# Attention scores of a gated linear attention: full-height products of a bank first, half-height products after

## The chip, the cores and the metric

The kernel runs on one core of a Trainium2 chip. The metric is the device time in microseconds of one execution; the kernel before was run three times. One further execution was taken with the hardware profiler, and all rows below come from its trace.

## The reference

Three stages follow each other: a gated linear attention over 4 x 8 heads, 768 tokens and 48 features; a gated product with shared weights; and a second layer in which each of the 3072 tokens goes to one of eight experts.

```python
# attention: q, k, v, f_logit are [4, 8, 768, 48]
f = 1.0 / (1.0 + np.exp(-f_logit))
for t in range(S):
    state = f[:, :, t, :, None] * state + np.einsum('bhd,bhe->bhde', k[:, :, t], v[:, :, t])
    y[:, :, t] = np.einsum('bhd,bhde->bhe', q[:, :, t], state)
# first MoE: x is y as [3072, 384], w_a and w_b [384, 1536], w_out [1536, 384]
x = ((x @ w_a) * (x @ w_b)) @ w_out
# second MoE: the expert of a token is the argmax of x @ w_gate, E = 8, F = 1024
for e in range(E):
    h = np.maximum(x[mask] @ w1[e], 0.0)
    out[mask] = gate_w[mask, None] * eom[mask, e, None] * (h @ w2[e])
```

## The kernel before, in words

**Tiles.** The 3072 tokens are 24 tiles of 128: six chunks of each of the four sequences. A tile goes through 14 steps of attention, and two tiles make a block of the first MoE. Numbers that need float32 precision are held as a high and a low part, so that most products come in three.

**One tile of attention.** The eight heads stand in four pairs. The step `a_z` writes the decayed q and k in half precision into the tile `z`: of a pair, q's high part twice for each head, q's low part, k high and low, k low and high. Each part has 64 columns per head, 48 of them used. A DMA transpose (L667) turns `z` into `zT`, in which a pair's two heads stand on the lower and the upper 64 partitions, or a head's high and low parts on both.

**The scores.** `a_score(i, u)` makes the scores of the four heads with number u in their pairs. They fill one bank of PSUM: four stretches of 128 columns, one for each pair j, in the bank tile `ps_at`. Each stretch is the sum of two products. L726 multiplies k (high and low, on all 128 partitions) with q's high part that stands on both halves: a product over 128 rows of TensorE's array. L727 multiplies k's high part on 64 of the partitions with q's low part on the same 64: a product over 64 rows. In the trace the former has the form 128*128, the latter 64*128. Both load weights of their own first (LDWEIGHTS, engine PEld in the profile).

**What follows a bank.** VectorE multiplies it with the causal mask into `sm` (L729), ScalarE makes the high part `Sh` (L731), VectorE the low part `Sl` (L732). L742 to L744 multiply these with v (`a_av`), L758 and L760 bring in the state before the chunk (`a_inter`), and L698 to L700 update the state (`a_kv`). The last of these use half of the array's columns, form 128*64.

**The first MoE.** `m_ab` (L816 to L818) multiplies a block with two column tiles of the weights, 256 columns at a time; `m_out` (L840 to L842) multiplies the result with `w_out`, 400 columns at a time.

**Order.** The first six tiles and first two blocks are laid out by a table of nominal times, while weights arrive and are decoded. From then on a loop over blocks j and weight tiles f calls `m_ab`, `m_out` and, by a table of steps, the attention of tiles 2j+2 and 2j+3. A scheduler then sets the order within each engine; it may put other work between two instructions of the program. Each engine works strictly through its list.

Of the kernel before, what the change touches and what calls it, by code (L numbers as in the profile page):

```python
# [18 lines left out]
DRAM = bass.MemoryType.DRAM  # L19
# [3 lines left out]
def general_path(nc, tc, q, k, v, f_logit, w_a, w_b, w_out, w_gate, w_ogate, w1, w2, out, cons):  # L23
    """the whole computation again, for values that the fast path doesn't carry"""
# [11 lines left out]
    with ExitStack() as ctx:  # L36
# [9 lines left out]
        # ---- recurrence over the tokens, one by one  # L46
# [52 lines left out]
        # ---- first MoE and the routing, 128 tokens at a time  # L99
        with tc.tile_pool(name="g_m1", bufs=1) as sp:  # L100
# [4 lines left out]
            for nm, w, n, m in (("a", w_a, KD, FF), ("b", w_b, KD, FF), ("o", w_out, NF, DM)):  # L105
                wt[nm] = tl("g_w" + nm, [P, n, m])
                for kk in range(n):
                    for c in range(m // DM):
                        cs = slice(c * DM, (c + 1) * DM)
                        src = w[kk * P : (kk + 1) * P, cs]  # L110
                        dst = wt[nm][:, kk, cs]
                        if w.dtype != I64:
                            nc.sync.dma_start(dst, src)
                            continue
                        raw = tl("g_raw", [P, DM, 2], I32)
                        nc.sync.dma_start(raw.bitcast(I64).rearrange("p f c -> p (f c)"), src)
                        top, low = raw[:, :, 1], raw[:, :, 0]
                        ei = tl("g_ei", [P, DM], I32)
                        ef = tl("g_ef", [P, DM])
                        mi = tl("g_mi", [P, DM], I32)  # L120
                        bits = dst.bitcast(I32)
                        nc.vector.tensor_scalar(
                            out=ei, in0=top, scalar1=20, scalar2=0x7FF,
                            op0=ALU.logical_shift_right, op1=ALU.bitwise_and,
                        )
                        nc.vector.tensor_copy(out=ef, in_=ei)
                        nc.vector.tensor_scalar(
                            out=ef, in0=ef, scalar1=896.0, scalar2=0.0, op0=ALU.subtract, op1=ALU.max
                        )
                        nc.vector.tensor_scalar(out=ef, in0=ef, scalar1=254.0, scalar2=None, op0=ALU.min)  # L130
                        nc.vector.tensor_copy(out=ei, in_=ef)
                        nc.vector.tensor_scalar(
                            out=ei, in0=ei, scalar1=23, scalar2=None, op0=ALU.logical_shift_left
                        )
                        nc.vector.tensor_scalar(
                            out=mi, in0=top, scalar1=3, scalar2=0x7FFFFF,
                            op0=ALU.logical_shift_left, op1=ALU.bitwise_and,
                        )
                        nc.vector.scalar_tensor_tensor(
                            out=mi, in0=low, scalar=29, in1=mi,  # L140
                            op0=ALU.logical_shift_right, op1=ALU.bitwise_or,
                        )
                        nc.vector.tensor_tensor(out=mi, in0=mi, in1=ei, op=ALU.bitwise_or)
                        nc.vector.scalar_tensor_tensor(
                            out=bits, in0=top, scalar=-(1 << 31), in1=mi,
                            op0=ALU.bitwise_and, op1=ALU.bitwise_or,
                        )
                        # below float32's range: zero
                        nc.vector.tensor_scalar(
                            out=ef, in0=ef, scalar1=1.0, scalar2=None, op0=ALU.min  # L150
                        )
                        nc.vector.tensor_tensor(out=dst, in0=dst, in1=ef, op=ALU.mult)
# [94 lines left out]
        # ---- the experts, 128 slots at a time  # L247
# [57 lines left out]
def kernel(  # L305
# [46 lines left out]
    # ---------------------------------------------------------------- pools  # L352
# [17 lines left out]
    # ------------------------------------------------------------ constants  # L370
    # n(t): number of steps of the static slope up to token t of a chunk
# [72 lines left out]
    # routing state: (token, scale) per token, counts, sums of the softmax, ranges  # L444
# [9 lines left out]
    # DRAM scratch: rows of the first MoE by token (and a row of zeros), slot table  # L454
# [6 lines left out]
    # ---------------------------------------------------- weights, hi and lo  # L461
# [16 lines left out]
    def decoded(raw, n, on_pool):  # L478
        """384 columns of a weight as float32, times 2^WS"""
# [7 lines left out]
        # The upper word as a float has the double's exponent over 8. Times 2^(WS - 126) its  # L487
        # three upper exponent bits are clear, as long as the double is below 2^(128 - WS):
        # the sums tell. Below 2^(-112 - WS) it comes to nothing.
# [34 lines left out]
    def conv_o(f, raw, n, on_pool):  # L524
# [7 lines left out]
        # w_out @ [w_gate | w_output_gate] for these rows  # L532
# [18 lines left out]
    # -------------------------------------------------------------- attention  # L551
# [15 lines left out]
    # Heads in pairs, the first of a pair on the lower 64 partitions and the second on the upper:  # L567
    # of a pair, q hi twice for each head, q lo, k hi and lo, k lo and hi
# [11 lines left out]
    def part(o):  # L580
        """the partitions of the pairs' first or second heads"""
        return slice(64 * o, 64 * o + D)
# [27 lines left out]

    def squares(i, n, src, scale, junk):
        """the sum of squares of every token's row"""
        nc.scalar.activation(
            out=junk, in_=src, func=AF.Square, scale=scale, accum_out=st_qkv[:, i, n : n + 1]
        )
# [55 lines left out]
    def a_u(i):  # L671
        """the state before this chunk, hi and lo"""
# [43 lines left out]
    def a_score(i, u):  # L716
# [6 lines left out]
        for j in range(4):  # L723
            half = slice(64 * u, 64 * u + 64)
            k2, ql = T[:, 5 * j + 3 + u], T[half, 5 * j + 2]
            nc.tensor.matmul(sc[:, j], k2, T[:, 5 * j + u], start=True, stop=False)  # L726
            nc.tensor.matmul(sc[:, j], k2[half], ql, start=False, stop=True)  # L727
# [38 lines left out]
    def a_turn(i):  # L766
        """rows to columns by DMA, two bytes at a time: the words' lower and upper halves apart"""
# [37 lines left out]
    # -------------------------------------------------------------- first MoE  # L805
# [81 lines left out]
    def r_rank(j):  # L887
        """every token's slot: its expert's base and the tokens before it"""
# [19 lines left out]
    def free_order(key, ins):  # L908
        """scatters of one table go to rows of their own: they don't wait for each other"""
# [50 lines left out]
    # ------------------------------------------------------- experts' weights  # L960
# [3 lines left out]
    def load_expert(e, g, part):  # L964
        """two f-tiles of the e-th expert in line: part 0 of w1, part 1 of w2"""
# [23 lines left out]
    # --------------------------------------------------- program, first phase  # L989
# [10 lines left out]
    def route(j, f):  # L1000
        """the tokens of block j, sent to their experts in steps"""
# [50 lines left out]
    # the first two blocks run while the weights come: emission by nominal time  # L1052
# [41 lines left out]
    # -------------------------------------------------------------- second MoE  # L1094
    # The experts stand in a line: first the one with the most tokens before the last block, then
    # the others by their number of tokens, most first, each place with slots of its own number.
    # No token of the last block goes to the first half of the first place's slots, so these can
    # start before that block ends.
# [14 lines left out]
    def tiles_of(e):  # L1113
        """tiles of the e-th place: first slot and size"""
# [12 lines left out]
    def choose_first():  # L1127
        """the expert with the most tokens before the last block gets the first place"""
# [24 lines left out]
    def first_tokens(n):  # L1153
        """half n of the first place's slots"""
# [17 lines left out]
    def e_turn(e, u):  # L1172
        """rows to columns by DMA, two bytes at a time: the words' lower and upper halves apart"""
# [50 lines left out]
    def e_h(e, f, n=None):  # L1224
        """the first product of the e-th place for f, or of half n of the first place"""
# [4 lines left out]
        # hi, then lo with the tokens of a pair first: both parts of these stand together  # L1230
# [17 lines left out]
    def is_pair(m):  # L1248
        """a tile so small that both parts of h stand beside each other in one product"""
        return m in (P // 4, P // 2)  # L1250
# [55 lines left out]
    def line_up(pc):  # L1306
        """the experts in their line, and whether one has too many tokens for its place"""
# [46 lines left out]
    def check_path():  # L1354
        """anything that the fast path doesn't carry: values out of its range or overfull experts"""
# [36 lines left out]
    def ahead(e, turn, columns, f):  # L1392
        """the input of the e-th place, while the one before is computed"""
# [6 lines left out]
    # ------------------------------------------------------------- the program  # L1400
# [137 lines left out]
```

## Time and profile before

| | |
|---|---|
| median of three runs | 931.11 us (930.51 to 933.27) |
| the profiled execution, its span | 931.4 us |
| mean granted TensorE clock | 0.974 of full speed |
| TensorE matmul busy | 862.8 us, 93%, 6733 instructions |
| VectorE, ScalarE, GpSimd busy | 549.6, 448.0 and 360.0 us |

A matmul's busy time holds its passage through the array, which overlaps that of the next one; how fast products follow each other is read from the distance of their starts. Times in rows are counted from the start of the profiled span. An arrow in brackets names what ended the engine's idle time before a row.

### The profile page before, as it was taken

How to read it: one execution, taken by the hardware profiler on the slowest of the kernel's cores; microseconds unless marked ns; L12 is line 12 of the kernel's file. 1: busy time of each engine (PE TensorE's matmuls, PEld its weight loads, DVE VectorE, ACT ScalarE, POOL GpSimd, SP SyncE). 2: the span in 40 equal slices, each digit the busy share in tenths (PEclk: the TensorE clock that was granted, in tenths of full speed). 3: DMA queues.
4: the chain of work that ended last, by engine and by line, in shares of the span. 5: the costliest groups of instructions: out<-in, count | busy, mean ns of one | idle time of the engine just before them, and what ended most of it. 6: DMA issues, size and time to landing. Idle time of an engine off the chain costs nothing.

```text
span 931.4 us, 18145 instructions
## 1 busy us (share of the span) xinstructions
PE 862.8 (93%) x6733; PEld 797.7 (86%) x6733; DVE 549.6 (59%) x1289; ACT 448.0 (48%) x1104; POOL 360.0 (39%) x428
## 2 busy tenths in 40 slices
PE   2689789989999999999999999999978999999993
PEld 1477789978989898989899999999878999999993
DVE  8887875554746474646555565642546666666630
ACT  6756655533545454536454554432424434445530
POOL 4444664352535353535445363412344231131111
PEclk9997999989999999999999999999989999999997
DMA  9874535462516252443526161211348644665610
GB/s 202 186 167 137 158 89 111 88 69 55 107 38 122 38 116 44 90 71 57 95 43 117 36 124 20 60 33 50 122 120 225 172 125 159 189 175 155 185 58 22
DMA packets 247756, 98.53 MB, mean 106 GB/s; under 512 B 210600, under 2 KB 243717, under 8 KB 247658
## 3 DMA queue, kind: packets, MB, share of 16 engines
q1 hardware_dynamic: 242538, 87.22, 42.3%
q0 software_dynamic: 4320, 10.03, 3.5%
q8 instruction: 55, 0.90, 0.4%
q14 instruction: 43, 0.35, 0.1%
q10 hardware_dynamic: 800, 0.02, 0.1%
HBM read 63.56 MB, written 10.49 MB: 80 GB/s over the span
## 4 chain that ended last, share of the span: by engine, by line
PE 70%; DMA 9%; DVE 8%; issue 7%; ACT 2%; POOL 2%; SPq 0%; POOLq 0%; DVEq 0%; ACTq 0%
PE ps_ab L816 9%; PE ps_ab L817 9%; PE ps_ab L818 9%; PE ps_out L301 5%; PE ps_out L842 4%; PE ps_out L841 4%; PE ps_yk L301 4%; PE ps_out L840 4%; PE ps_ab L1221 3%; PE ps_ab L1220 3%; PE ps_ab L1222 3%; PE ps_at L727 3%; PE ps_at L726 3%; DMA slots<-info,di 2%; DMA zT<-z 2%
## 5 line engine op out<-in xcount | busy, mean ns | idle before, releaser
L816 PE MATMUL ps_ab<-xh,wab 128*128 128x256 f32 x864 | 253.0, 293 | 5.5 <-DVE gf L824 3.8
L817 PE MATMUL ps_ab<-xl,wab 128*128 128x256 f32 x864 | 248.8, 288 | 0.5 <-DVE xl L797 0.5
L818 PE MATMUL ps_ab<-xh,wab 128*128 128x256 f32 x864 | 248.5, 288 | 0.2 <-POOL wab L520 0.2
L828 POOL TENSOR_TENSOR gl<-gf,gh 128x256 fp32r<-128x256 f32 x144 | 111.6, 777 | 244.7 <-ACT gh L827 243.3
L816 PEld LDWEIGHTS ps_ab<-xh,wab 128*128 128x128 f32 x864 | 167.1, 194 | 9.4 <-DVE gf L824 4.7
L817 PEld LDWEIGHTS ps_ab<-xl,wab 128*128 128x128 f32 x864 | 167.1, 193 | 2.3 <-DVE xl L797 1.8
L818 PEld LDWEIGHTS ps_ab<-xh,wab 128*128 128x128 f32 x864 | 167.2, 193 | 0.7 <-POOL wab L520 0.3
L824 DVE SCALAR_TENSOR_TENSOR gf<-ps_ab,asb 128x256 f32<-128x256 f32 x144 | 60.3, 419 | 81.4 <-ACT asb L823 76.0
L827 ACT ACTIVATE gh<-gf 128x256 fp32r<-128x256 f32 x144 | 59.9, 417 | 93.4 <-DVE gf L824 90.0
L841 PE MATMUL ps_out<-wo,gh 128*128 128x400 f32 x264 | 93.0, 352 | 2.2 <-DVE wo L547 2.2
L842 PE MATMUL ps_out<-wo,gl 128*128 128x400 f32 x264 | 92.2, 357 | 2.2 <-POOL gl L828 2.2
L840 PE MATMUL ps_out<-wo,gh 128*128 128x400 f32 x264 | 89.9, 348 | 1.3 <-ACT wo L546 1.3
L1294 POOL DMA_INDIRECT out_dram<-ys,tab x29 | 30.0, 1033 | 145.4 <-ACT ys L1289 139.9
L823 ACT ACTIVATE asb<-ps_ab 128x256 f32<-128x256 f32 x144 | 54.4, 379 | 58.1 <-PE ps_ab L818 57.9
L1221 PE MATMUL ps_ab<-xsl,wab 128*128 128x256 f32 (+5 forms) x216 | 73.5, 341 | 0.1
L1220 PE MATMUL ps_ab<-xsh,wab 128*128 128x256 f32 (+5 forms) x216 | 73.5, 341 | 0.1
L1222 PE MATMUL ps_ab<-xsh,wab 128*128 128x256 f32 (+5 forms) x216 | 73.3, 339 | 0.0
L977 DVE TENSOR_TENSOR wab<-raw,wab 128x768 fp32r<-128x768 f32 x48 | 46.6, 972 | 40.4 <-ACT wab L301 40.0
L1234 ACT ACTIVATE h<-ps_ab 128x256 fp32r<-128x256 f32 (+5 forms) x72 | 34.7, 483 | 69.3 <-PE ps_ab L1222 64.6
L1238 DVE SCALAR_TENSOR_TENSOR h<-ps_ab,h 128x64 fp32r<-128x64 f32 (+5 forms) x96 | 41.1, 450 | 36.7 <-ACT h L1234 36.7
L729 DVE TENSOR_TENSOR sm<-ps_at,mask 128x512 f32<-128x512 f32 x48 | 33.0, 688 | 45.0 <-PE ps_at L727 44.8
L732 DVE TENSOR_TENSOR Sl<-sm,Sh 128x512 f16<-128x512 f32 x48 | 33.9, 706 | 40.0 <-ACT Sh L731 40.0
(261 smaller groups left out, 1977.7 us busy)
## 6 DMA issues: line engine op xcount, KB each, us to landing
raw<-in_moe_w_dram SPq DMA_DIRECT2D x64, 384.0 KB
in_f<-in_f_logit_dram SPq DMA_DIRECT2D x24, 192.0 KB
in_q<-in_q_dram SPq DMA_DIRECT2D x24, 192.0 KB
in_k<-in_k_dram SPq DMA_DIRECT2D x24, 192.0 KB
in_v<-in_v_dram SPq DMA_DIRECT2D x24, 192.0 KB
raw<-in_moe_w_a_dram SPq DMA_DIRECT2D x12, 384.0 KB
raw<-in_moe_w_b_dram SPq DMA_DIRECT2D x12, 384.0 KB
raw<-in_moe_w_out_dram SPq DMA_DIRECT2D x12, 384.0 KB
```

The source lines that it names most:

```text
L301: return lambda *a, **k: tc.keep_in_program_order(op(*a, **k))
L816: nc.tensor.matmul(pab[:, a], wh[:, kk, o : o + P], xh[:, kk], start=(kk == 0), stop=False)
L817: nc.tensor.matmul(pab[:, a], wh[:, kk, o : o + P], xl[:, kk], start=False, stop=False)
L818: nc.tensor.matmul(pab[:, a], wl[:, kk, o : o + P], xh[:, kk], start=False, stop=(kk == KD - 1))
L824: nc.vector.scalar_tensor_tensor(out=gf, in0=pab[:, 1], scalar=2.0**-WS, in1=asb, op0=ALU.mult, op1=ALU.mult)
L828: nc.gpsimd.tensor_tensor(out=gl, in0=gf, in1=gh.bitcast(F32), op=ALU.subtract)
L840: nc.tensor.matmul(o, gh[:, ts], wh[:, u], start=(f == 0), stop=False)
L841: nc.tensor.matmul(o, gh[:, ts], wl[:, u], start=False, stop=False)
L842: nc.tensor.matmul(o, gl[:, ts], wh[:, u], start=False, stop=(f == NF - 1))
L1220: nc.tensor.matmul(ph, wh[:, kk, o : o + P], sh[:, kk, us], start=(kk == 0), stop=False)
L1221: nc.tensor.matmul(ph, wh[:, kk, o : o + P], sl[:, kk, us], start=False, stop=False)
L1222: nc.tensor.matmul(ph, wl[:, kk, o : o + P], sh[:, kk, us], start=False, stop=(kk == KD - 1))
```

## The change

In a bank the four products over 128 rows now come first, one for each pair, and the four products over 64 rows behind them. The first product clears the accumulation state of the bank (`start`), the last one closes it (`stop`); before, each stretch had a `start` and a `stop` of its own. Each product is tied behind the one before it by a dependency without a semaphore, so that the scheduler keeps the eight in this sequence. Comments and doc strings were dropped elsewhere in the file, which shifts line numbers: both products are now made in line 741.

```diff
+    def queued_behind(ins, before):
+
+        tc.add_manual_dep(
+            ins.ins,
+            before.ins.name,
+            mybir.DependencyInfo(mybir.DependencyClass.NoSync, mybir.DependencyReason.DATA),
+            reason="one group of a bank",
+        )
...
-        for j in range(4):
-            half = slice(64 * u, 64 * u + 64)
-            k2, ql = T[:, 5 * j + 3 + u], T[half, 5 * j + 2]
-            nc.tensor.matmul(sc[:, j], k2, T[:, 5 * j + u], start=True, stop=False)
-            nc.tensor.matmul(sc[:, j], k2[half], ql, start=False, stop=True)
+
+        half = slice(64 * u, 64 * u + 64)
+        before = None
+        for part in range(2):
+            for j in range(4):
+                k2, q2 = T[:, 5 * j + 3 + u], T[:, 5 * j + u]
+                if part == 1:
+                    k2, q2 = k2[half], T[half, 5 * j + 2]
+                first_of, last_of = part + j == 0, part + j == 4
+                ins = nc.tensor.matmul(sc[:, j], k2, q2, start=first_of, stop=last_of)
+                if before is not None:
+                    queued_behind(ins, before)
+                before = ins
```

TensorE's list around one bank of the loop over blocks, before: the last product of `m_ab`, then the bank's products over 128 rows (L726) and 64 rows (L727) in turn, then `a_av`.

```order
L816 MATMUL ps_ab<-xh,wab 128x256
L726 LDWEIGHTS zT
L726 MATMUL ps_at<-zT 128x128
L727 LDWEIGHTS zT
L727 MATMUL ps_at<-zT 128x128
L726 LDWEIGHTS zT
L726 MATMUL ps_at<-zT 128x128
...
L727 LDWEIGHTS zT
L727 MATMUL ps_at<-zT 128x128
L742 LDWEIGHTS Sh
```

The same place in the changed kernel; L741 makes all eight pairs of rows, of which the first four are over 128 rows and the last four over 64.

```order
L833 MATMUL ps_ab<-xh,wab 128x256
L741 LDWEIGHTS zT
L741 MATMUL ps_at<-zT 128x128
...
L741 LDWEIGHTS zT
L741 MATMUL ps_at<-zT 128x128
L759 LDWEIGHTS Sh
```

Only the sequence inside the bank moved; the rows ahead of it and behind it are the same. With line numbers matched, the lists of all five engines and the waits in them are otherwise as before.

One bank of the 48 (tile 20, u = 0) has other work inside. Before, its first three products stand ahead of a stretch of `m_ab` and `m_out`, the other five behind it. The start of the stretch and its end, before:

```order
L900 MATMUL ps_at<-oh,stri 128x8
L726 LDWEIGHTS zT
L726 MATMUL ps_at<-zT 128x128
L727 LDWEIGHTS zT
L727 MATMUL ps_at<-zT 128x128
L726 LDWEIGHTS zT
L726 MATMUL ps_at<-zT 128x128
L816 MATMUL ps_ab<-xh,wab 128x256
...
L842 MATMUL ps_out<-wo,gl 128x400
L727 LDWEIGHTS zT
L727 MATMUL ps_at<-zT 128x128
L726 LDWEIGHTS zT
```

In the changed kernel the same slots are taken, three products ahead and five behind:

```order
L917 MATMUL ps_at<-oh,stri 128x8
L741 LDWEIGHTS zT
L741 MATMUL ps_at<-zT 128x128
...
L833 MATMUL ps_ab<-xh,wab 128x256
...
L859 MATMUL ps_out<-wo,gl 128x400
L741 LDWEIGHTS zT
L741 MATMUL ps_at<-zT 128x128
```

The three ahead are now over 128 rows, and of the five behind the first is over 128 rows and four over 64.

## Rows read from the trace of the kernel before

**Rows 1.** Busy us (instructions) of each engine, clock, DMA share, GB/s by stage

```profile
0.00:130.00 130.00, 91.06 (x674) 73.78 (x674) 110.96 (x232) 83.14 (x229) 65.42 (x81) 0.93 0.69 167
130.00:616.00 486.00, 480.51 (x4315) 442.45 (x4316) 274.29 (x689) 239.64 (x639) 214.28 (x269) 0.99 0.41 74
```

**Rows 2.** Waits of PE, 130 to 616 us: total, times, longest

```profile
PE ps_yk L742 <- ACT Sh L731: 3.2, 1, 3.2
PE ps_at L726 <- DMA zT<-z: 1.2, 2, 0.7
```

**Rows 3.** Line L726 before 130 us and from 130 to 616: ns min/median/max

```profile
L726 PE MATMUL ps_at<-zT x32: 216/289/330, 18.4 to 76.1; 128*128 128x128 f16 x32
...
L726 PE MATMUL ps_at<-zT x160: 216/230/230, 146.3 to 609.8; 128*128 128x128 f16 x160
```

**Rows 4.** PE in order of time around one bank: start, duration, instruction

```profile
300.33 0.34 PE L840 MATMUL ps_out<-wo,gh 128*128 128x400 f32 x1
...
300.70 0.34 PE L842 MATMUL ps_out<-wo,gl 128*128 128x400 f32 x1
300.96 0.22 PE L698 MATMUL ps_at<-vs,z 128*64 128x48 f16 x2
...
301.33 0.19 PE L700 MATMUL ps_at<-vs,z 128*64 128x48 f16 x1
301.45 0.23 PE L726 MATMUL ps_at<-zT 128*128 128x128 f16 x1
301.62 0.23 PE L727 MATMUL ps_at<-zT 64*128 64x128 f16 x1
301.78 0.23 PE L726 MATMUL ps_at<-zT 128*128 128x128 f16 x1
...
302.58 0.23 PE L727 MATMUL ps_at<-zT 64*128 64x128 f16 x1
302.74 0.39 PE L816 MATMUL ps_ab<-xh,wab 128*128 128x256 f32 x1
```

**Rows 5.** PE around 425 us, 17 products left out; weight loads of L743

```profile
425.12 0.19 PE L744 MATMUL ps_yk<-vv,Sl 128*128 128x48 f16 x1
...
425.58 0.18 PE L744 MATMUL ps_yk<-vv,Sl 128*128 128x48 f16 x1
...
L743 PEld LDWEIGHTS <-Sh 128*128 128x128 f16 x192 | 17.0, 99 | 0.1
```

**Rows 6.** PE in order of time in tile 3's second bank

```profile
76.11 0.29 PE L726 MATMUL ps_at<-zT 128*128 128x128 f16 x1
76.33 0.29 PE L727 MATMUL ps_at<-zT 64*128 64x128 f16 x1
```

**Rows 7.** Chain that ended last: 60 to 80, 76 to 90, 130 to 616 us

```profile
by line: DMA zT<-z 24.7%; PE ps_at L727 15.1%; PE ps_at L726 14.2%; PE ps_ab L818 8.0%; PE ps_out L841 6.5%; PE ps_ab L816 6.1%; PE ps_ab L817 6.0%; PE ps_out L842 5.0%; PE ps_at L545 3.5%; PE ps_at L787 3.2%; PE ps_out L840 3.2%; PE ps_yk 
...
86.31 4.11 DMA raw<-in_moe_w_a_dram
...
by line: PE ps_ab L816 15.8%; PE ps_ab L817 15.2%; PE ps_ab L818 15.0%; PE ps_out L842 7.1%; PE ps_out L841 7.0%; PE ps_out L840 6.9%; PE ps_at L727 5.0%; PE ps_at L726 4.6%; DMA zT<-z 3.4%; DMA slots<-info,di 2.4%; issue 1.6%; PE ps_yk L74
...
197.04 11.77 DMA slots<-info,di
```

**Rows 8.** PE in order of time: starts of tile 6's two banks

```profile
195.78 0.23 PE L726 MATMUL ps_at<-zT 128*128 128x128 f16 x1
...
200.43 0.23 PE L726 MATMUL ps_at<-zT 128*128 128x128 f16 x1
```

**Rows 9.** ACT, PE and SP's queue in order of time, tiles 14 and 15

```profile
402.82 0.63 ACT L731 ACTIVATE Sh<-sm 128x512 f16<-128x512 f32 x1 [1.04 <-DVE sm L729]
...
406.28 0.20 PE L742 MATMUL ps_yk<-vv,Sh 128*128 128x48 f16 x1
...
406.97 4.01 SPq L667 DMA_TRANSPOSE zT<-z  x1
...
413.06 0.23 PE L726 MATMUL ps_at<-zT 128*128 128x128 f16 x1 [0.47 <-DMA zT<-z]
```

## The prediction

> **What bounds the kernel now.** I read first the busy table by stage [rows 1]. The reader is to see two stages in it and a third behind them: up to 130 us TensorE (PE) is busy 91.1 of 130 us and VectorE (DVE) 111.0; from 130 to 616 us PE is busy 480.5 of 486 us, while DVE has 274.3 and the others less; after that the second MoE runs, which has no attention score in it. Then I read what PE waits for in the middle stage [rows 2]: its two largest waits come to 4.4 us, and all of its idle time there is 486 - 480.5 = 5.5 us. So between 130 and 616 us whatever PE does not have to do comes off the time, unless a wait takes its place. The list of one line's instructions gives where the score products lie: 160 of the 192 products over 128 rows stand in that stage, 32 before it [rows 3]. A bank has four of them, so there are 40 banks in the middle stage (token tiles 4 to 23) and 8 before it (tiles 0 to 3).
>
> Next I read PE in order of time around one bank [rows 4]. A matmul's duration there (0.23 us) is a latency that overlaps the next one; what counts is the distance between starts. From L726 to L727 it is 0.17 us and from L727 to the next L726 0.16: the bank takes from 301.45 to 302.74, that is 1.29 us or 0.16 us for each product of 128 columns. Compare the neighbours. Two steps between products of 400 columns take 0.37 us (300.33 to 300.70, same rows; the one between them is left out), 0.46 ns for a column; 128 columns should take 59 ns by that. In the products over all 128 rows of L742 to L744, 48 columns wide, 18 distances take from 425.12 to 425.58, 25.6 ns each, each with a weight load of its own that lasts 99 ns [rows 5]. So weight loads as such lie beside the stream, and adding to a place in the bank that was written just before costs nothing either (these three lines do that too). What is peculiar to the score bank is that it changes, at every step, between the whole array (128 rows) and half of its rows (64).
>
> The kernel has one other place with such a change, and it tells the price [rows 4]: the products of L698 to L700 use half of the array's columns (128*64). The first of them starts 0.26 us after a product of 400 columns instead of 0.18 to 0.19, and the product over the whole array behind the last of them starts 0.12 us later (301.33 to 301.45) instead of 0.03. Inside the half-array stretch twelve rows, most of two products, one on each half, take from 300.96 to 301.33: 0.034 us from one to the next. So entering or leaving a form costs some 70 to 90 ns, and staying in it costs nothing.
>
> **The change part by part.** No instruction is added or removed: each bank has the same eight weight loads and eight matmuls, and in the built order every other row of every engine, with its waits, stands where it stood. The added dependencies tie instructions of one engine to each other and put no wait into the program. The clear of the bank by the first product alone, in place of four clears, is a flag of the same instruction; I cost it at nothing. What changes is the number of changes of form. Before, a bank enters and leaves the half form four times (F h F h F h F h): 8 changes. After (F F F F h h h h): 2.
>
> Cost of one bank before, at the full clock: four entries of 162 ns and four exits of 158 ns (to two digits 0.17 and 0.16 in [rows 4]) = 1280 ns, against the 1290 read there. After: three steps F to F, one F to h at 162, three steps h to h, one exit at 158. F to F: from below 59 ns (the 0.46 ns of a column), from above 25.6 x 128 / 48 = 68 ns [rows 5]; I take 59, since the 25.6 ns hold a part that does not grow with the columns. h to h does not stand in the trace at all. From below it is 59 ns; from above it is the 162 ns of today's entry, if a weight load into half of the rows can't lie beside a product of the same half. I take 59, by the nearest row: in the half-column form of [rows 4] each half of the array has a new product with new weights every 0.034 us. A bank is then 6 x 59 + 162 + 158 = 674 ns, and the gain 1280 - 674 = 606 ns. At half the clock (the second bank of tile 3, [rows 6]) a step is 0.22 us, and 128 columns take twice 59, that is 118: the gain is 6 x 102 = 612 ns.
>
> Where it counts. The chain that ended last between 130 and 616 us holds 9.6% in L726 and L727 [rows 7], 46.7 us of the 40 x 1.28 = 51.2 us: nearly all banks are on it. I leave out the two of tile 6, which start at 195.78 and 200.43 [rows 8]: behind them PE stands idle for 3.2 us for Sh [rows 2], and the chain goes through a scatter that lands after 11.77 us [rows 7]. That gives 38 x 0.606 = 23.0 us.
>
> Of the first stage, tiles 0 and 1 bring nothing: the stage is DVE's. Tiles 2 and 3 are on the chain (29.3% of the 20 us from 60 to 80, 5.9 us, is their four banks [rows 7]): 2 x 0.606 + 2 x 0.612 = 2.4 us. But from 86 us on that chain goes through loads of weights and their decoding, which were partly issued earlier and do not all move with it. I take half, 1.2 us, with 0 and 2.4 as the ends.
>
> What could take it back: a product that arrives sooner waits for what has not become faster. Sh of a bank comes from DVE and ScalarE; in the steady stretch it is ready at 403.45 (402.82 + 0.63) and first used at 406.28 [rows 9], a slack of 2.83 us in which one other bank lies, so 2.2 us are left. The transpose zT of the odd tile lands when PE wants it, without slack (issued 406.97, first used 413.06, PE idle 0.47 us for it). Its issue follows PE's last read of the tile's single buffer, and no score bank stands between that read and the use; the wait stays as it is and moves along. Behind 616 us everything starts from PE's last products and moves along too.
>
> Sum: 23.0 + 1.2 = 24.2 us. The profiled execution's span is 931.4 us, the median of the three runs 931.1; they agree within the 0.3% that a measurement of this kernel can tell from no change, so I take the sum off the median: **906.9 us**.
>
> **The rivals.** *The h to h steps stay at 162 ns,* because all four use the same 64 rows and a weight load into rows that are streaming must wait. Then only the three F to F steps gain, 3 x 101 = 303 ns a bank: 38 x 0.303 + 0.6 = 12.1 us, 919.0 us. For it: nothing in this kernel runs two such products in a row. Against it: the loads of 99 ns in [rows 5] do lie beside products that use the same rows. The Trainium skill, "TensorE: Matmul & The Clock Gate", section "Part 3: Packing small matmuls — row/col tiling", has a rule that speaks for this rival: a weight load overlaps running matmuls only where its row group differs. Taken strictly it would deny the F to F steps their gain as well; there the trace disagrees with it (25.6 ns a product beside loads of 99), and for half the rows no run here shows it yet.
>
> *Nothing changes,* because the 160 ns belong to the products and not to the alternation: 931 us. For it: each L727 is followed late, whatever comes behind it. Against it: a product over the whole array behind the half-column form has the same kind of surcharge, and L727 itself streams no more columns than L726.
>
> *Slower:* a product over half of the rows has to drain its own predecessor completely, load and stream, and so costs more than today's step. The gain of the F to F steps (303 ns) is used up when h to h costs 162 + 101 = 263 ns; the largest distance into a half form in [rows 4], 0.26 us behind 400 columns, would come near that. Slower by 0.3% (2.8 us over 38 banks, 74 ns a bank) it would be from 288 ns on: 934 us. Nothing in the trace reaches it.
>
> **How the numbers follow.** Forecast (both kinds of steps flow, or h to h a little dearer): 0.84. Only F to F gains: 0.09. No change: 0.04. Slower: 0.03. The first two are faster by over 0.3%, 0.93 together; within 0.3% is 0.04, slower 0.03. The range: below, all 40 banks at 606 ns and the whole early part give 24.2 + 2.4 = 26.6 us, 904.5, and if the 4.4 us of waits in [rows 2] go as well, 900. Above, h to h at 115 ns, between its two ends, leaves 3 x 101 + 3 x 45 = 438 ns, 38 x 0.438 = 16.6 us, 914.5. So 900 to 914 us, with the three rivals outside.
>
> **What would show it.** In the profile after: starts inside a bank 59 ns apart except one step of 0.16 us in the middle; a bank of 0.67 us up to the next line's start; still 0.16 us from its last product to the next line. PE's waits in the middle stage stay near 6 us. It is wrong if h to h steps are over 0.1 us, if new waits for Sh, zT or the decoded weights add up to more than 5 us, or if the early stage ends no sooner although its banks are shorter.

## The result and the profile after

The changed kernel takes 908.2 us (median of four runs, 906.3 to 911.4), the kernel before 932.2 in the same comparison: a ratio of 0.974, 95% interval 0.971 to 0.977, some 24 us. The profiled execution has a span of 909.6 us (before 931.4).

First, PE around two banks of the changed kernel, in order of time (start, duration, instruction). Consecutive rows of one line are merged, so the duration of a merged row reaches from its first start to its last end.

```profile
393.34 0.40 PE L741 MATMUL ps_at<-zT 128*128 128x128 f16 x4
393.67 0.39 PE L741 MATMUL ps_at<-zT 64*128 64x128 f16 x4
394.00 0.22 PE L707 MATMUL ps_at<-vs,z 128*64 128x48 f16 x2
...
295.32 0.72 PE L741 MATMUL ps_at<-zT 128*128 128x128 f16 x8
295.97 0.38 PE L833 MATMUL ps_ab<-xh,wab 128*128 128x256 f32 x1
```

The reader is to see three things. Four products over all rows (F) take 0.40 us with 0.22 us for the last one, so their three steps share 0.18 us; by the starts in the trace they are 67, 55 and 56 ns. The four over 64 rows (h) have the same steps, 67, 55 and 56 ns. And the whole bank takes 0.65 us to the next line's start (295.32 to 295.97), where [rows 4] have 1.29. What is left of the bank at 393.34 are its two changes of form: 152 ns from the last F to the first h (393.67), and 146 ns from the last h to the next line (394.00).

The weight loads of the same bank show why the 64-row products flow:

```profile
393.34 0.23 PEld L741 LDWEIGHTS <-zT 128*128 128x128 f16 x4 [0.18 <-issue]
393.67 0.22 PEld L741 LDWEIGHTS <-zT 64*128 64x128 f16 x4
...
L741 PEld LDWEIGHTS <-zT x320: 92/96/106, 142.0 to 587.5; 128*128 128x128 f16 x80, 64*128 64x128 f16 x80
```

Four loads of 92 to 106 ns each (the last row: least, median and most from tile 4 on) end within 0.22 to 0.23 us: they overlap each other and the products, within 64 rows just as within 128. In the kernel before, each load starts together with its own product ([rows 4]) and 0.16 us behind the load before it:

```profile
301.45 0.10 PEld L726 LDWEIGHTS <-zT 128*128 128x128 f16 x1
301.61 0.09 PEld L727 LDWEIGHTS <-zT 64*128 64x128 f16 x1
301.77 0.10 PEld L726 LDWEIGHTS <-zT 128*128 128x128 f16 x1
```

So the load of the other form is what comes late at a change; what TensorE does in that time no row shows.

In tile 3 the granted clock is 0.50 in both kernels, the level of 1.2 GHz. Its second bank ([rows 6]) takes 1.12 us (71.86 to 72.98) where it took 1.79 (74.75 to 76.54); its first one takes 1.08 us (68.37 to 69.45). First the kernel before:

```profile
74.75 0.33 PE L726 MATMUL ps_at<-zT 128*128 128x128 f16 x1
...
76.54 0.70 PE L841 MATMUL ps_out<-wo,gh 128*128 128x400 f32 x1
```

The changed kernel:

```profile
68.37 1.14 PE L741 MATMUL ps_at<-zT 128*128 128x128 f16 x8 [0.25 <-DMA zT<-z]
69.45 0.22 PE L761 MATMUL ps_yk<-vv,Sl 128*128 128x48 f16 x1
...
71.86 1.19 PE L741 MATMUL ps_at<-zT 128*128 128x128 f16 x8
72.98 0.70 PE L858 MATMUL ps_out<-wo,gh 128*128 128x400 f32 x1
```

The busy table by stage answers [rows 1]; the middle stage now ends some 22 us earlier, at 594 us.

```profile
0.00:130.00 130.00, 89.89 (x703) 76.67 (x704) 114.69 (x236) 85.17 (x235) 69.18 (x85) 0.93 0.70 167
130.00:594.00 464.00, 453.17 (x4293) 427.76 (x4292) 271.32 (x684) 237.55 (x634) 210.31 (x266) 0.99 0.43 77
```

PE's idle time there is 464 - 453.2 = 10.8 us, where it was 5.5. What it waits for, all six rows of that view, answers [rows 2]:

```profile
PE ps_at L741 <- DMA zT<-z: 8.7, 5, 3.6
PE ps_yk L759 <- ACT Sh L748: 0.5, 1, 0.5
PE ps_yk L761 <- DVE Sl L749: 0.5, 1, 0.5
PE ps_at L761 <- DVE Sl L749: 0.4, 1, 0.4
PE ps_ab L833 <- DVE gf L841: 0.4, 1, 0.4
PE ps_at L759 <- ACT Sh L748: 0.3, 1, 0.3
```

The 3.2 us for Sh are gone and the waits for zT are longer; how much of that is due to the change is told below, with the runs that keep the old turns. Two of the waits for zT are large, at tiles 6 and 7; the wait of tile 15, which answers to [rows 9], is now 0.92 us.

```profile
193.65 0.72 PE L741 MATMUL ps_at<-zT 128*128 128x128 f16 x8 [3.63 <-DMA zT<-z]
210.89 0.83 PE L741 MATMUL ps_at<-zT 128*128 128x128 f16 x8 [3.38 <-DMA zT<-z]
...
401.44 0.23 PE L741 MATMUL ps_at<-zT 128*128 128x128 f16 x1 [0.92 <-DMA zT<-z]
```

### The profile page after: what moved, and what is told of

It is laid out like the page before. It is cut to its first block, busy times and chain, and to the rows that moved or that the text cites. A ratio compares the mean times of both kernels' runs of the same rounds, so it can differ in the third digit from the quotient of the medians.

```text
span 909.6 us, 18145 instructions
## 1 busy us (share of the span) xinstructions
PE 833.1 (92%) x6733; PEld 784.0 (86%) x6733; DVE 550.5 (61%) x1289; ACT 447.8 (49%) x1104; POOL 359.3 (39%) x428
## 4 chain that ended last, share of the span: by engine, by line
PE 62%; DMA 12%; DVE 10%; issue 7%; ACT 4%; POOL 2%; SPq 2%; POOLq 0%; DVEq 0%; ACTq 0%
PE ps_ab L833 9%; PE ps_ab L834 8%; PE ps_ab L835 8%; PE ps_out L301 4%; PE ps_out L859 4%; PE ps_out L858 4%; PE ps_out L857 4%; PE ps_yk L301 4%; DMA zT<-z 3%; PE ps_ab L1237 3%; PE ps_ab L1238 3%; PE ps_ab L1239 3%; DMA in_f<-in_f_logit_dram 3%; PE ps_at L741 2%; DMA raw<-in_moe_w_dram 2%
## 5 line engine op out<-in xcount | busy, mean ns | idle before, releaser
L301 ACT ACTIVATE wab<-raw 128x768 fp32r<-128x768 f32 x48 | 40.4, 842 | 34.6 <-DMA raw<-in_moe_w_dram 34.3
```

The costliest lines, as they stand in the source:

```text
L301: return lambda *a, **k: tc.keep_in_program_order(op(*a, **k))
```

## Experiments

Theory A: a change between the whole array and half of its rows has a price, and only the number of changes counts. Against it stood that the price lies in the groups with a clear and an end of their own (B), in adding to the stretch that the product just before wrote (C), or in the 64-row product itself (D). All runs below keep the order of every other instruction. In each the loop became a list of (pair, part) in the wanted order:

```diff
-        for part in range(2):
-            for j in range(4):
+        turns = [...]
+        for n, (j, part) in enumerate(turns):
...
-                first_of, last_of = part + j == 0, part + j == 4
-                ins = nc.tensor.matmul(sc[:, j], k2, q2, start=first_of, stop=last_of)
+            ins = nc.tensor.matmul(sc[:, j], k2, q2, start=(n == 0), stop=(n == 7))
```

**Old turns, new flags and ties (8 changes).**

```diff
+        turns = [(j, part) for j in range(4) for part in range(2)]
```

> The products keep the old turns (F h F h F h F h), but with the changed kernel's flags and ties: one clear for the bank, eight products tied in sequence. Theory A (each change between the whole array and half of its rows costs about 104 ns; 8 changes as before): a bank of 1.28 us, the time of the kernel before, within 0.3%. Theory B (the price lay in the four groups with a clear and an end each): a bank of 0.65 us and the changed kernel's time, a ratio of 0.974 to before.

Measured: 932.5 us, ratio 0.9995 (0.997 to 1.002). The bank, in order of time:

```profile
355.72 1.35 PE L740 MATMUL ps_at<-zT 128*128 128x128 f16 x8
357.01 0.22 PE L707 MATMUL ps_at<-vs,z 128*64 128x48 f16 x2
```

1.28 us by the starts in the trace, as before. Flags and ties do nothing by themselves; theory B falls.

**Two and two (4 changes).**

```diff
+        turns = [(2 * g + j, part) for g in range(2) for part in range(2) for j in range(2)]
```

> The turns are F F h h F F h h: 4 changes in place of 8 or 2, and no product right behind another one into the same stretch of the bank. Theory A: 0.65 + 2 x 0.104 = 0.86 us a bank, two thirds of the changed kernel's gain, about 915 us, ratio 0.983. Theory C (the price lay in adding a product to the stretch that the one just before it wrote): 0.65 us a bank as in the changed kernel, ratio 0.974. Theory D (a product over 64 rows is dear by itself): no change between 8, 4 and 2 changes would be seen at all.

Measured: 917.3 us, ratio 0.985 (0.981 to 0.988). The bank:

```profile
347.78 0.93 PE L740 MATMUL ps_at<-zT 128*128 128x128 f16 x8
348.64 0.22 PE L707 MATMUL ps_at<-vs,z 128*64 128x48 f16 x2
```

0.86 us, on the expected value. No product here adds right behind another one to the same stretch, and still the bank is dearer than in the changed kernel: C does not explain it. Nor does D, since the number of 64-row products is the same in all three.

**All rows, old turns (no change inside a bank).** The low product takes all 128 rows, and so adds a term of low times low to the scores.

```diff
+        turns = [(j, part) for j in range(4) for part in range(2)]
...
-                    k2, q2 = k2[half], T[half, 5 * j + 2]
+                k2, q2 = k2, T[:, 5 * j + 2]
```

> Old turns, but the low product takes all 128 rows too (it adds the product of the low part of k with the other head's low part of q, so the scores differ by terms of the size of low times low). Theory A: no change of form in a bank, 8 x 56 ns = 0.45 us, 0.83 us less than before: 40 banks give 33 us and the time is about 897 us, or up to 903 where waits for zT grow (8.7 us in the changed kernel's profile). Theory C: the alternation alone is dear, 1.28 us a bank, 931 us.

Measured: 902.0 us, ratio 0.967 (0.964 to 0.971).

```profile
341.47 0.62 PE L740 MATMUL ps_at<-zT 128*128 128x128 f16 x8
342.02 0.22 PE L707 MATMUL ps_at<-vs,z 128*64 128x48 f16 x2
```

The duration of 0.62 us is seven steps of 55 to 67 ns and one product of 0.22. This bank takes 0.55 us, since the line behind it has the half-column form: 0.15 us pass from the last start to its first. Most banks of this run are followed by a product over the whole array and take 0.42 to 0.46 us, as expected. The old alternation is harmless once both products have one form, and so is adding to the stretch that was written just before: C falls with this run.

**All rows, new turns.**

```diff
+        turns = [(j, part) for part in range(2) for j in range(4)]
...
-                    k2, q2 = k2[half], T[half, 5 * j + 2]
+                k2, q2 = k2, T[:, 5 * j + 2]
```

> The changed kernel's sequence with all eight products over 128 rows (the same added terms of low times low as in the run with the old turns). Theory A: the sequence no longer matters, 0.45 us a bank, the same time as with the old turns within 0.3%, some 8 us below the changed kernel if waits for zT don't take it. Theory C: only here is the bank short, and the run with the old turns is about 30 us slower.

Measured: 901.0 us, ratio 0.967 (0.963 to 0.970), the same as with the old turns. This pair is the fastest seen here: some 6 us below the changed kernel, at the price of the added term.

**The change in one stage alone.** My sum gave the first stage 1.2 us, and the first bank of tile 4 starts 4.4 us earlier in the changed kernel (141.98 against 146.33). Two runs split the change:

```diff
+        turns = [(j, part) for part in range(2) for j in range(4)] if i < 4 else [(j, part) for j in range(4) for part in range(2)]
```

> The new sequence only in the 8 banks of tiles 0 to 3, the old turns in the other 40. Theory A with the bound read from the trace (the first stage waits for VectorE and weights): at most 2.4 us faster than before, likely about 1, within the noise; the first bank of tile 4 starts 0 to 2.4 us earlier than in a kernel with the old turns. Theory E (the first stage follows TensorE after all, and the 4.4 us by which the changed kernel's tile 4 started earlier are of the change): some 4 us faster, ratio 0.996.

Measured: 931.4 us, ratio 0.995 (0.992 to 0.998), that is 4.7 us with an interval from 2.1 to 7.2. Theory E's 4 us lie in it, of theory A's 0 to 2.4 us only the upper end. The profiled execution of this run does not show the gain at the end: its tile 4 starts 3.3 us before that of the kernel before, its tile 8 only 0.2 us, and its last bank at the same time (next table).

```diff
+        turns = [(j, part) for part in range(2) for j in range(4)] if i >= 4 else [(j, part) for j in range(4) for part in range(2)]
```

> The new sequence in the 40 banks of tiles 4 to 23 alone. Theory A: nearly the whole gain, 40 x 0.626 = 25 us less what waits for zT and for the scatter around tile 6 take, some 20 to 23 us; ratio 0.975 to 0.979. Theory E: 4 us less than the changed kernel gains, ratio 0.979 or above while the changed kernel has 0.974.

Measured: 911.6 us, ratio 0.974 (0.969 to 0.978), that is 24.7 us with an interval from 20.5 to 28.8, as much as the whole change. The interval is too wide to tell the two theories apart; the starts of the banks in the next table are sharper, but of one execution each.

**The changed kernel again.**

> The changed kernel once more, beside the two that apply it to one stage. Bank of 0.654 us again; ratio 0.974. Open is how large the waits of TensorE for zT and Sh around tiles 6 and 7 are this time (7.0 us for zT in the first profile, 4.4 us in all in the kernel before): if they are chance of one execution, they differ by microseconds from that; if the shorter banks cause them, they are again near 7 us and about 3 us above those of a kernel with the old turns.

Measured: 907.2 us, ratio 0.972 (0.967 to 0.976). PE's waits from 130 us to the end of the middle stage, the two largest rows of the view:

```profile
PE ps_at L741 <- DMA zT<-z: 8.3, 3, 4.5
PE ps_at L761 <- DVE Sl L749: 0.4, 1, 0.4
```

Again near 8 us for zT. With old turns in tiles 4 to 23 it is 6.1 us in the run with new flags and 6.2 in the one with only the early tiles changed:

```profile
PE ps_at L740 <- DMA zT<-z: 6.1, 3, 3.3
PE ps_yk L760 <- DVE Sl L748: 0.2, 1, 0.2
```

So among the three profiles with old turns there, the kernel before, with 1.2 us for zT and 3.2 for Sh, is the odd one. At tile 6 PE waits 0, 3.3 and 4.1 us for zT with old turns (where it is 0, the 3.2 us for Sh follow) and 3.6, 4.5 and 4.5 with new ones: nearly the same. At tile 7 it waits 0.7, 2.2 and 1.3 us with old turns and 3.4, 3.6 and 2.9 with new ones. The rows of that wait, old turns first (the kernel before, the runs with new flags and with the early tiles changed), then the run with tiles 4 to 23 changed and the repetition:

```profile
214.87 0.23 PE L726 MATMUL ps_at<-zT 128*128 128x128 f16 x1 [0.72 <-DMA zT<-z]
213.79 1.35 PE L740 MATMUL ps_at<-zT 128*128 128x128 f16 x8 [2.20 <-DMA zT<-z]
213.19 1.45 PE L740 MATMUL ps_at<-zT 128*128 128x128 f16 x8 [1.28 <-DMA zT<-z]
217.12 0.72 PE L740 MATMUL ps_at<-zT 128*128 128x128 f16 x8 [3.64 <-DMA zT<-z]
209.58 0.72 PE L741 MATMUL ps_at<-zT 128*128 128x128 f16 x8 [2.88 <-DMA zT<-z]
```

SP's queue shows what tile 7's transpose stands behind, first in the kernel before, then in the changed one: a load `g<-gd` that is issued only 8.0 and 7.5 us after the store `gd<-eq`. From that store to PE's first use of tile 7's zT pass 13.9 us before and 13.4 after.

```profile
200.97 0.39 SPq L645 DMA_DIRECT2D gd<-eq  x1
209.00 0.82 SPq L678 DMA_DIRECT2D g<-gd  x2
209.99 3.08 SPq L667 DMA_TRANSPOSE zT<-z  x1
...
197.48 0.39 SPq L654 DMA_DIRECT2D gd<-eq  x1
205.02 0.82 SPq L687 DMA_DIRECT2D g<-gd  x2
206.00 3.10 SPq L676 DMA_TRANSPOSE zT<-z  x1
```

The starts of three score banks, read from the order of time of each profile (us; "last" is tile 23's second bank):

| turns | tile 4 | tile 8 | last | tile 4 to last | tile 8 to last |
|---|---|---|---|---|---|
| before | 146.33 | 251.86 | 608.83 | 462.5 | 357.0 |
| old turns, new flags | 144.48 | 252.34 | 609.22 | 464.7 | 356.9 |
| new in tiles 0 to 3 | 143.03 | 251.66 | 608.84 | 465.8 | 357.2 |
| new in tiles 4 to 23 | 147.92 | 254.39 | 592.89 | 445.0 | 338.5 |
| changed | 141.98 | 248.14 | 587.05 | 445.1 | 338.9 |
| changed again | 141.06 | 245.37 | 583.43 | 442.4 | 338.1 |
| two and two | 141.76 | 247.98 | 592.28 | 450.5 | 344.3 |
| all rows, old turns | 141.55 | 245.00 | 577.22 | 435.7 | 332.2 |
| all rows, new turns | 141.74 | 245.37 | 577.19 | 435.5 | 331.8 |

In the first six rows, tile 4 starts at 146.2 us on average where tiles 0 to 3 have the old turns and at 142.0 where they have the new ones: 4.2 us, with a spread of 3.4 and 2.0 us within the three. From tile 4 to the last bank it is 464.3 against 444.2 us: 20.1 us. The stretch from tile 8 on has next to no spread: 357.0, 344.3, 338.5 and 332.0 us with 8, 4, 2 and no changes in a bank.

## Why the prediction was right, point by point

**The bank.** Predicted 674 ns, measured 654 (0.65 in the rows above). The six steps F to F and h to h take 356 ns (67, 55 and 56 twice), for which I had taken 6 x 59 = 354; the 20 ns too many lie in the two changes of form, 152 and 146 ns in place of 162 and 158. The choice that h to h flows, by the nearest row, the half-column form, was the step on which all hung, and it was right. The runs with 8, 4 and 2 changes give 1280, 862 and 654 ns, so 104 ns for each change, the same between any two of the three. The Trainium skill, "TensorEngine Tiling (Array Packing)", section "Tiling Modes", says that changing the tiling mode drains TensorE; the trace agrees in so far as every change has a price here, these 104 ns, but no row shows a drain.

**The rival of h to h.** It falls: loads into the same 64 rows lie beside the products of these rows. The Trainium skill's rule that a load overlaps only products of another row group ("TensorE: Matmul & The Clock Gate", section "Part 3: Packing small matmuls — row/col tiling") is not what the rows here show: 55 to 67 ns from product to product with loads of 92 to 106 ns. The rival of no change falls with the pair that uses all rows, and the slower one would have needed an h to h step of more than 263 ns.

**The middle stage.** Predicted 38 x 0.606 = 23.0 us, measured 20.1 over its 39 steps from bank to bank. PE itself saves more than I said, 40 x 0.626 = 25.0 us, the banks of tile 6 included, 24.4 in 39 steps. What failed is the step that let PE's waits stay as they are: all rows of that view come to 10.8 us in the changed kernel, 9.5 in its repetition and 11.4 in the run with new turns from tile 4 on, against 5.9 before and 6.3 and 6.2 in the two runs with old turns there. That is some 4.4 us given back, which closes the sum: 24.4 - 4.4 = 20.0. The prediction had named new waits of more than 5 us as a sign that it is wrong; with 4.9 us more than in the profile before it comes to the edge of that.

The three runs with new turns share it, so it is not chance of one execution. Most of it lies between tiles 4 and 8, where of 8 x 0.626 = 5.0 us only 1.7 come through. From tile 8 on 18.5 of 31 x 0.626 = 19.4 us do, so in the steady stretch the slack that was counted from one pair of tiles ([rows 9]) nearly holds. The largest part, 1.9 us on average, is the wait at tile 7. There the transpose does not follow PE's last read of the buffer, as I had it for an odd tile: that read ends at 201.8 us in the changed kernel, and the transpose is issued at 206.0, behind the store and the load ahead of it in SP's queue, a chain that takes nearly as long as before (13.4 and 13.9 us). That this chain is the cause is read from the rows; no run tested it. At tile 6 waits of 3.3 and 4.1 us stand in runs with old turns too; why zT or Sh comes late there was not tried.

**The first stage.** Predicted 1.2 us, with 2.4 as the upper end; measured 4.2 by the start of tile 4 and 4.7 (2.1 to 7.2) by the run with the change there alone. The step that failed is "I take half", on the ground that the chain goes on through loads and decoding. The four banks that I counted save 2 x 0.63 at the full clock and 2 x (1.76 - 1.08) at the low one, 2.6 us. That this came through whole is not shown: with four changes in a bank, and with none, tile 4 starts at 141.6 to 141.8 us as well, so its start does not follow the length of the banks. The granted clock may move it too. The latest start, 147.92, is of an execution with a mean granted clock of 0.89 in the first 130 us where the others of the six have 0.92 to 0.93, and in the run with new turns in tiles 0 to 3 both banks of tile 3 ran at the full clock (0.65 us each). How much of the 4.2 us the shorter banks make stays open.

**The sum.** 20.1 + 4.2 = 24.3 us against 24.2 predicted, and 24.0 measured. The two mis-sized terms, 3 us too many in the middle and 3 too few in front, cancel, and that is luck: the time of 906.9 us is nearer to the 908.2 than its terms deserve. The split itself is known to some 3 us only, the spread of the starts of tile 4. Behind the last bank nothing changed: 931.36 - 608.83 = 322.5 us before and 909.60 - 587.05 = 322.6 after.

## What to carry to other kernels

Read the distance of starts, not the duration, and compare it with a neighbour of the same width: a product that takes 160 ns for 128 columns where 56 would do is waiting for something. Where products of different array forms alternate, sort them so that each form stands in one run; where the smaller product can take all rows and the added terms do no harm, that saves the last changes as well (some 6 us here), since a 64-row product streams no faster than a 128-row one. Of time taken off a busy engine, expect a part back as waits for transfers whose latency did not shrink (4 of 25 us here).

## What the runs showed of the hardware

A change between the whole array and half of its rows cost 104 ns at the full clock (granted clock 1.00, 2.4 GHz), about the same on entry and on exit. A product over 64 rows with 128 columns costs as much as one over 128 rows, 55 to 67 ns from start to start. I had not expected that leaving the half form costs what entering it does, nor that the price hardly depends on the clock: at the granted clock of 0.50 (1.2 GHz) eight steps of 0.22 us, 1.76 us, become 1.08 us with six changes fewer, 113 ns a change, while a step without one goes from 56 to 107 ns.
